# A pair of 64-row matmuls moved behind the convolution's visits, and into layer 1, in an S4D and channel-MLP kernel

## The chip, the core and the metric

The kernel runs on one core of a Trainium2 chip. The metric is the device time of one execution in microseconds (us). TensorE is called PE here, VectorE DVE, ScalarE ACT, GpSimd POOL and SyncE SP, as in the profile. A matmul has weights (the stationary operand, at most 128x128) and a moving operand whose columns stream past them; the profile writes the shape of the weights ahead of the matmul's own shape, as in `64*128 64x512`.

## The reference

```python
x = A_u                                   # (1, 2048, 576)
xn = layernorm(x)
# s: state-space convolution, per channel, with a kernel K made from 128 complex states
A = -exp(log_A_real) + 1j * A_imag;  C = (C_real + 1j * C_imag) * dt[:, None]
K = 2 * einsum("dn,dnl->dl", C, exp(A * dt * pos)).real
s = irfft(rfft(xn, 2L) * rfft(K, 2L))[:L] + xn * D_skip
# g: silu of a channel MLP, 576 -> 4608 -> 576
h = gelu(layernorm(xn) @ w1 + b1)
g = silu(h @ w2 + b2)
return x + s * g
```

All of it is float32.

## The kernel before

**The MLP.** It is most of PE's work. It runs in 48 slots: two halves of the tokens, in each 12 groups of 384 hidden columns, in each two blocks of 512 tokens. Float32 operands are split into a high and a low part, so that a product takes three matmuls (high x high, low x high, high x low). Layer 1 of a slot (L633) has three blocks of 128 hidden columns (i = 0, 1, 2). The contraction over 576 channels is four chunks of 128 rows, three matmuls each, and a rest of 64 rows. For the rest, `XR` holds the high part of the tokens in rows 0 to 63 and the low part in rows 64 to 127. One matmul with the weights `w1r` (the high part, twice) and one with `w1s` (the low part, twice) finish the block: 14 matmuls of 512 columns in all. Behind each block ACT takes gelu (L671) and the high part `hh` (L674), and DVE takes the low part `hl` (L677). Layer 2 (L707) multiplies these with `w2` in 72 matmuls of 288 columns, for four tiles of 128 tokens, and DVE adds each tile to `acc` (L717). Two PSUM buffers, `mxa` and `mxb`, alternate.

**The pair.** Of the `w1s` matmul only the 64 rows of the weights' low part by the tokens' high part are needed. A pair (L616) does that for blocks 0 and 2 of a slot by two matmuls of 64 rows side by side: one reads rows 0 to 63 of `XR`, the other a copy of them in rows 64 to 127 of `XQ` (named `bias` in the profile), fetched by a DMA in the slot before. These two start blocks 0 and 2, which then have 13 matmuls each. Pairs are made only where a slot begins behind a visit to the convolution, and stand ahead of that visit.

**The convolution** uses the PSUM buffer `cv`, in small matmuls that come as visits between blocks of the MLP. A visit has one or two segments of these kinds: kgen (L1042, weights of 128x32, 36 of them), x1 (L1157, 64x128, 12), k1 (L1188, 32x128, 12), s2 (L1217, 64x32, 24), inv (L1260, 32x64, 12), i1 (L1286, 128x64, 6). ACT and DVE take the results out and prepare the next operands.

**The order.** `Order` writes out the order of each engine's instructions beforehand, with its own clock and durations, and pins it. `pe_turns`, called behind blocks of the MLP, decides whether a visit stands there: by `EDGE`, `END`, `ALONE` and `DUE`, and by the positions at which visits are looked for (`all_lines`). `ride` puts a waiting kgen into another visit. `HOLD` names single steps of ACT and DVE that are traced one or two instructions later on their engine than the planner would have them.

**The end.** In the last slots, outputs are finished tile by tile: ACT takes the silu (L802), DVE multiplies (L809 or L811 and L815) and adds `u` (L820), DMAs store. The first half of the outputs comes out by `combine`: POOL's queue loads three tiles of rows (L746 to L748), DVE multiplies and adds (L754, L755), POOL's queue stores (L758). For the last chunk of channels this is done in three sets, of 3, 3 and 2 tiles, each behind the set before it, from the moment the last i1 is stored (L1295).

Of the kernel before, what the change touches and what calls it, by code (L numbers as in the profile page):

```python
# [18 lines left out]
P = 128  # L19
# [13 lines left out]
G = 3  # L33
# [191 lines left out]
def mixer_kernel(ctx, tc, u, log_a_real, a_imag, c_real, c_imag, log_dt, d_skip, w1, b1, w2, b2,  # L225
                 f1, f2, g2, g1, tvals, ident, out, parts=("mlp", "s4d")):
    nc = tc.nc
# [6 lines left out]
    def bank2(name):  # L234
        return ps.tile([P, 2, TB], F32, name=name, bufs=2 if name == "cv" else 1)
# [165 lines left out]
    MV, SECOND, PAIR, M4, SINGLE = {}, [], {}, [], {}  # L401
# [70 lines left out]
    XR = sb.tile([P, 2, TB], F32R, name="XR")  # L472
    XQ = {}
# [58 lines left out]
    W = {}  # L532
# [56 lines left out]
    HID, LAST, Q1, Q2, IDM = {}, {}, {}, {}, []  # L589
    turn = [0]  # L590

    def mx(i):
        return "mxa" if (turn[0] + i) % 2 == 0 else "mxb"

    BEGUN = set()
# [10 lines left out]
            XQ[0] = sb.tile([P, D], F32R, name="bias2")[:, :TB]  # L606
        nc.sync.dma_start(XQ[0][64:].bitcast(F32), XR[:64, tb].bitcast(F32))

    def pair(tb):

        Q1[0] = bank2(mx(1))
        for e, x in enumerate((XR[:64, tb], XQ[0][64:])):
            r, k = slice(64 * e, 64 * e + 64), e * (G - 1)
            nc.tensor.matmul(Q1[0][:, e], W[1][3][r, k * P:(k + 1) * P], x, start=True, stop=False,  # L616
                             skip_group_check=True)
        BEGUN.update((0, G - 1))

    def layer1(g, tb, i):  # L620
        h, lo, r1, r2 = W[1]
# [331 lines left out]
    def tables(b):  # L953
# [37 lines left out]
        def weigh(part):  # L991
# [10 lines left out]
            else:  # L1002
# [14 lines left out]
                + [step("DVE", dve((2, 2, 1, 1)[part] * n), f(weigh, part), need=[("sin", b, 1)],  # L1017
                        mark=("wu", b) if part == 3 else None, hold=HOLD.get(("weigh", b, part), 0)) for part in range(4)])

# [49 lines left out]
        return behind  # L1069


    X1, S2, INV, I1, KG = 1.5, 1.75, 2.15, 3.05, 1.03

    HOLD = {("weigh", 19, 3): 1, ("phase", 19): 1, ("frac", 18): 2, ("k", 2, 1): (2, 1), (2, 0, 24): 1, (2, 1, 24): 1, ("k1", 2, 1, 2): 1}

    def chunk(c):

# [240 lines left out]
    NPOS = G + 8  # L1318
    NSLOT = 4 * NG
    od = Order(tc, nc)  # L1320
    od.pinned = True
    el, wl2, wl, nl2, pl, pl2, nl, ml, ml2, xl, wx, c3, c2, c1, c4, kl, tl, sl, vl, gl, odl, fl = [od.line() for _ in range(22)]
    nlh, mlh, mlt = od.line(), od.line(), od.line()
    od.lines = od.lines[-3:] + od.lines[:-3]

# [75 lines left out]
    od.pin()  # L1401


    L1 = 14 * 0.2315
    LEN = [L1] * G + [3 * n * 0.132 + 0.02 for n in (4, 2, 2, 4, 3, 3, 3, 3)]

    T0 = 12.5
    for e, t in dict(PE=0.0, ACT=4.6, DVE=3.7, POOL=3.8, SP=0.0).items():
# [98 lines left out]
    def wmark(n, which):  # L1507

        per = KB + 1 + G
        a = n * per + (0 if which == 1 else KB + 1)  # L1510
        return [("w", k) for k in range(a, a + (KB + 1 if which == 1 else G))]
# [63 lines left out]


    pace = dict(left=NCH * (2 + 2 + 4), last=0.0, started=False)
    END = 1000.0


    EDGE = 0.2, 0.6
    ALONE, DUE = 20.0, (160.0, 950.0)

    def pe_turns(limit=1, any_time=False, all_lines=True, edge=None):
        for x in (nl, pl, ml) + ((c3, c1, kl) if all_lines else ()):
            n = 0
            while n < (2 if x in (c1, nl) else limit):
                h = od.head(x)
                if h is None or h[0]["eng"] != "PE" or h[1] > od.t["PE"] + (0.3 if x is nl else -0.4):
                    break  # L1590
                if x is c1:
                    now = od.t["PE"]
                    gap = (END - now) / max(pace["left"], 1)
                    if n == 0 and pace["started"] and now < pace["last"] + EDGE[edge is None] * gap and not any_time:
                        break
                    pace["started"], pace["last"] = True, now
                    pace["left"] -= 1
                if x is kl and pace["started"]:
                    b = kl["steps"][0]["mark"][1]
                    wait = ("wu", b + 1) not in od.marks or od.t["PE"] < DUE[0] + b * (DUE[1] - DUE[0]) / NB  # L1600
                    if b < NB - 1 and od.t["PE"] < h[1] + (ALONE if wait else 3.0):
                        break
                if edge is not None and not BEGUN and x in (c3, c1, kl):
                    m = wmark(edge // 2, 1) + [("xq", edge)]
                    if all(k in od.marks and od.marks[k] < od.t["PE"] - 0.3 for k in m):
                        od.unit(lambda: pair(edge % 2), 0.24)
                behind = ride(h[0]) if x in (c1, c3) else None
                od.run(x)
                if behind:
                    behind()  # L1610
                od.pin()
                od.advance(od.t["PE"])
                n += 1

    LATER = {}

    def later(slot, pos, f):
# [53 lines left out]
    for slot in range(NSLOT):  # L1671
        turn[0] = slot + 1
        od.shared = slot > 1
        g, tb = slot // 2 % NG, slot % 2
        n = slot // 2
        final = slot >= NSLOT - 2
        for pos in range(NPOS):
            if pos < G:
# [9 lines left out]
                if pos == 2:  # L1688
                    BEGUN.clear()
                    k = slot % (2 * NG)  # L1690
# [16 lines left out]
            else:  # L1707
# [13 lines left out]
                if halves:  # L1721
                    dh = terms[0][1]
                    od.marks["z", dh] = od.t["PE"] + od.LAT
                    x = od.line()
# [3 lines left out]
                if split:  # L1728
                    add = cell[0]
                    for d in range(2) if j == 0 else (terms[0][1],):  # L1730
                        m = ("acc", slot, j, d)
# [3 lines left out]
                        x = od.line()  # L1735
# [3 lines left out]
                if last and not halves:  # L1739
# [4 lines left out]
                    elif final:  # L1744
                        x = el if slot < NSLOT - 1 else od.line()
# [12 lines left out]
            for f in LATER.get((slot, pos), ()):  # L1758
                f()
            od.advance(od.t["PE"])  # L1760
            pe_turns(edge=slot + 1 if pos == NPOS - 1 else None, all_lines=pos in (0, 1, 2, G + 1, G + 3, G + 5, NPOS - 1))
    od.force(lambda: not od.urgent and not any(x["steps"] for x in od.lines))


# [52 lines left out]
```

## Time and profile before

| | before |
|---|---|
| median of 3 runs | 1095.55 us (1095.23 to 1095.94) |
| the profiled execution | 1095.67 us, of which its span 1093.9 us |
| granted PE clock | 0.999 |
| PE busy | 1087.1 us, 99% |
| DVE, ACT, POOL busy | 891.9 us (82%), 727.1 us (66%), 188.4 us (17%) |
| chain that ended last | PE 95%, DVE 3%, ACT 1% |
| pairs (L616) | 16 |

Matmuls overlap: of two in a row the second starts long before the profile's end of the first, so what a matmul costs PE is read from start to start and not from its duration. In the timeline, rows of one kind are merged (`x4`), and the first number is the start of the first of them.

### The profile page before, as it was taken

How to read it: one execution, taken by the hardware profiler on the slowest of the kernel's cores; microseconds unless marked ns; L12 is line 12 of the kernel's file. 1: busy time of each engine (PE TensorE's matmuls, PEld its weight loads, DVE VectorE, ACT ScalarE, POOL GpSimd, SP SyncE). 2: the span in 40 equal slices, each digit the busy share in tenths (PEclk: the TensorE clock that was granted, in tenths of full speed). 3: DMA queues.
4: the chain of work that ended last, by engine and by line, in shares of the span. 5: the costliest groups of instructions: out<-in, count | busy, mean ns of one | idle time of the engine just before them, and what ended most of it. 6: DMA issues, size and time to landing. Idle time of an engine off the chain costs nothing.

```text
span 1093.9 us, 27052 instructions
## 1 busy us (share of the span) xinstructions
PE 1087.1 (99%) x11445; PEld 954.0 (87%) x11445; DVE 891.9 (82%) x1302; ACT 727.1 (66%) x1113; POOL 188.4 (17%) x261
## 2 busy tenths in 40 slices
PE   9999999999999999999999999999999999999998
PEld 7989899899888898888988888888888888888897
DVE  7798667889998879889899987997969888766367
ACT  6585699778676674767767848685675757534333
POOL 4566210153020100001100000000001021101132
PEclk9999999999999999999999999999999999999999
DMA  8746764626354152355624215143142434454444
GB/s 242 225 149 152 236 235 143 179 80 157 116 160 134 44 112 67 96 110 148 161 48 118 78 56 141 34 122 87 56 126 42 144 101 132 114 170 150 137 151 103
DMA packets 139553, 138.22 MB, mean 126 GB/s; under 512 B 88952, under 2 KB 105016, under 8 KB 138856
## 3 DMA queue, kind: packets, MB, share of 16 engines
q1 hardware_dynamic: 124424, 85.05, 29.0%
q0 software_dynamic: 14528, 50.71, 14.7%
q8 instruction: 89, 1.46, 0.6%
q10 hardware_dynamic: 480, 0.74, 0.3%
q14 instruction: 32, 0.26, 0.1%
HBM read 102.17 MB, written 36.63 MB: 127 GB/s over the span
## 4 chain that ended last, share of the span: by engine, by line
PE 95%; DVE 3%; ACT 1%; SPq 1%; issue 0%; DMA 0%; POOL 0%; DVEq 0%; ACTq 0%; POOLq 0%
PE mxb L707 20%; PE mxa L707 20%; PE mxa L633 20%; PE mxb L633 20%; PE cv L1217 3%; PE cv L1042 3%; PE cv L1260 2%; PE cv L1286 2%; PE cv L1188 1%; PE cv L1157 1%; PE mxa L1348 1%; DVE acc L717 0%; PE mxa L648 0%; SPq L1089 0%; PE mxb L616 0%
## 5 line engine op out<-in xcount | busy, mean ns | idle before, releaser
L677 DVE TENSOR_TENSOR hl<-h,hh 128x512 fp32r<-128x512 f32 x144 | 98.5, 687 | 99.2 <-ACT hh L674 98.4
L707 PE MATMUL mxa<-w2h,hh 128*128 128x288 f32 x573 | 170.3, 297 | 0.0
L707 PE MATMUL mxb<-w2h,hh 128*128 128x288 f32 x573 | 170.2, 297 | 0.0
L707 PE MATMUL mxb<-w2h,hl 128*128 128x288 f32 x573 | 169.3, 295 | 0.1
L707 PE MATMUL mxa<-w2h,hl 128*128 128x288 f32 x573 | 169.1, 295 | 0.0
L707 PE MATMUL mxa<-w2l,hh 128*128 128x288 f32 x573 | 168.6, 294 | 0.0
L707 PE MATMUL mxb<-w2l,hh 128*128 128x288 f32 x573 | 168.6, 294 | 0.0
L671 ACT ACTIVATE h<-mxa,b1t 128x512 f32<-128x512 f32 x73 | 50.1, 687 | 98.3 <-PE mxa L633 95.1
L707 PEld LDWEIGHTS mxa<-w2h,hh 128*128 128x128 f32 x573 | 107.6, 188 | 5.8 <-issue 3.0
L707 PEld LDWEIGHTS mxb<-w2h,hh 128*128 128x128 f32 x573 | 107.6, 188 | 4.3 <-issue 1.4
L707 PEld LDWEIGHTS mxb<-w2l,hh 128*128 128x128 f32 x573 | 107.6, 188 | 0.8
L707 PEld LDWEIGHTS mxa<-w2l,hh 128*128 128x128 f32 x573 | 107.6, 188 | 0.6
L707 PEld LDWEIGHTS mxb<-w2h,hl 128*128 128x128 f32 x573 | 107.5, 188 | 0.3 <-DVE hl L677 0.3
L707 PEld LDWEIGHTS mxa<-w2h,hl 128*128 128x128 f32 x573 | 107.5, 188 | 0.0
L671 ACT ACTIVATE h<-mxb,b1t 128x512 f32<-128x512 f32 x71 | 48.8, 687 | 69.7 <-PE mxb L633 67.2
L674 ACT ACTIVATE hh<-h 128x512 fp32r<-128x512 f32 x144 | 90.7, 631 | 3.7
L944 POOL DMA_DIRECT2D par<-par_s x36 | 27.8, 771 | 367.8 <-DVE mg L988 325.0
L717 DVE TENSOR_TENSOR acc<-mxa,acc 128x576 f32<-128x576 f32 x87 | 65.5, 753 | 26.0 <-PE mxa L707 25.9
L717 DVE TENSOR_TENSOR acc<-mxb,acc 128x576 f32<-128x576 f32 (+1 forms) x89 | 65.9, 741 | 17.8 <-PE mxb L707 17.7
L633 PE MATMUL mxa<-XH,w1h 128*128 128x512 f32 x284 | 79.2, 401 | 0.0
L633 PE MATMUL mxb<-XH,w1h 128*128 128x512 f32 x280 | 77.7, 399 | 0.0
L633 PE MATMUL mxa<-XL,w1h 128*128 128x512 f32 x284 | 76.1, 390 | 0.0
(277 smaller groups left out, 2494.4 us busy)
## 6 DMA issues: line engine op xcount, KB each, us to landing
raw<-in_B_w_dram SPq DMA_DIRECT2D x72, 288.0 KB, 3.4
raw<-in_B_w_dram SPq DMA_DIRECT2D x96, 192.0 KB, 3.5
par_s<-A POOLq DMA_DIRECT2D x4, 2160.0 KB, 8.1
par<-par_s POOLq DMA_DIRECT2D x36, 240.0 KB, 3.6
f2t<-f2q SPq DMA_DIRECT2D x24, 256.0 KB, 3.6
g2t<-g2p SPq DMA_DIRECT2D x24, 256.0 KB, 4.1
bias<-XR SPq DMA_DIRECT2D x42, 128.0 KB, 3.6
raw<-in_B_w_dram SPq DMA_DIRECT2D x48, 96.0 KB, 3.7
```

The costliest lines, as they stand in the source:

```text
L633: nc.tensor.matmul(q, a, b, start=j == 0 and i not in BEGUN, stop=j == len(ops) - 1, skip_group_check=True)
L671: nc.scalar.activation(t, q, AF.Gelu_apprx_tanh, bias=b1t[:, k:k + 1], scale=1.0)
L674: LAST[0] = nc.scalar.activation(hh[:, i], t, AF.Copy)
L677: nc.vector.tensor_sub(hl[:, i], t, hh[:, i].bitcast(F32))
L707: nc.tensor.matmul(q[:, dh, :288], a[:, i, c], b[:, i, d], start=i == 0 and k == 0 and alone != 1, stop=i == G - 1 and k == 2, skip_group_ ...
L717: nc.vector.tensor_add(o, q[:, dh:dh + n, :288], b)
L944: nc.gpsimd.dma_start(PAR[b].rearrange("p (g i) k -> p g (i k)", g=4), dram(par_s, (b // 3 * 48 + b % 3 * 4) * NPAR, [[D * NPAR, P], [12 * ...
L1042: nc.tensor.matmul(q[32 * g:32 * g + 32, i // 2, i % 2 * 64:i % 2 * 64 + 64], U[:, ri, 4 * g + i, :], v[:, ri, 4 * g + i, :], start=ri == ...
L1157: nc.tensor.matmul(Q[24 * v][:, e], FP[0][r, f, 0], x[r, 12 * e:12 * e + 12], start=n == 0, stop=n == 2, skip_group_check=True)
L1217: nc.tensor.matmul(Q[i][32 * q:32 * q + 32, f, ri::2], m[r, 4 * i + q, 32 * ri:32 * ri + 32], A2[r, 4 * p + 2 * i + q // 2, :, :, q % 2], ...
L1260: nc.tensor.matmul(QI[q // 2][64 * f:64 * f + 64, q % 2, i], MAT["g2t", p + i // 2][r, i % 2, f, ri], YS[p + i // 2][0][r, i % 2, ri, f], ...
L1286: nc.tensor.matmul(Q[h][64 * y:64 * y + 64, t], g1t.rearrange("p a e -> p (a e)"), A2[:, k:k + 2, 1].rearrange("p i d r -> p i r d"), star ...
```

## The change

The pair now stands behind the visit and no longer ahead of it. It is also made within layer 1: where a visit stands behind block 0, a pair starts blocks 1 and 2 of the same slot. The planner takes 0.29 us for it, where it took 0.24 us. Beside this, nearly all settings of the order are new and `HOLD` is empty, so that visits stand in other places throughout the kernel; two lines of the planner (c2, c3 and c4, kl) change rank, and visits are no longer looked for at position G + 5.

```diff
-    def pair(tb):
+    def pair(tb, i):
-        Q1[0] = bank2(mx(1))
-        for e, x in enumerate((XR[:64, tb], XQ[0][64:])):
-            r, k = slice(64 * e, 64 * e + 64), e * (G - 1)
-            nc.tensor.matmul(Q1[0][:, e], W[1][3][r, k * P:(k + 1) * P], x, start=True, stop=False,
+        Q1[i] = bank2(mx(1))
+        for e, k, q, x in ((0, i, Q1[i][:, 0], XR[:64, tb]), (1, 2, Q1[0][:, 1], XQ[0][64:])):
+            nc.tensor.matmul(q, W[1][3][64 * e:64 * e + 64, k * P:(k + 1) * P], x, start=True, stop=False,
                              skip_group_check=True)
-        BEGUN.update((0, G - 1))
+        BEGUN.update((i, 2))
...
-    X1, S2, INV, I1, KG = 1.5, 1.75, 2.15, 3.05, 1.03
-    HOLD = {("weigh", 19, 3): 1, ("phase", 19): 1, ("frac", 18): 2, ("k", 2, 1): (2, 1), (2, 0, 24): 1, (2, 1, 24): 1, ("k1", 2, 1, 2): 1}
+    X1, S2, INV, I1, KG = 1.3, 1.73, 2.23, 2.96, 1.1
+    HOLD = {}
...
-    el, wl2, wl, nl2, pl, pl2, nl, ml, ml2, xl, wx, c3, c2, c1, c4, kl, tl, sl, vl, gl, odl, fl = [od.line() for _ in range(22)]
+    el, wl2, wl, nl2, pl, pl2, nl, ml, ml2, xl, wx, c2, c3, c1, kl, c4, tl, sl, vl, gl, odl, fl = [od.line() for _ in range(22)]
...
-    END = 1000.0
-    EDGE = 0.2, 0.6
-    ALONE, DUE = 20.0, (160.0, 950.0)
-    def pe_turns(limit=1, any_time=False, all_lines=True, edge=None):
+    END = 1005.0
+    EDGE = 0.01, 0.21
+    ALONE, DUE = 24.3, (97.0, 926.0)
+    PAIR, SOLO = (0.46, 0.29), False
+    def pe_turns(limit=1, any_time=False, all_lines=True, edge=None, to=None, inner=False):
+        away = 0
...
-                if edge is not None and not BEGUN and x in (c3, c1, kl):
-                    m = wmark(edge // 2, 1) + [("xq", edge)]
-                    if all(k in od.marks and od.marks[k] < od.t["PE"] - 0.3 for k in m):
-                        od.unit(lambda: pair(edge % 2), 0.24)
+                away += x in (c3, c1, kl)
                 behind = ride(h[0]) if x in (c1, c3) else None
                 od.run(x)
...
+        if (away or inner and SOLO) and to is not None and not BEGUN:
+            m = wmark(to // 2, 1) + [("xq", to)]
+            if all(k in od.marks and od.marks[k] < od.t["PE"] - 0.3 for k in m):
+                od.unit(lambda: pair(to % 2, int(inner)), PAIR[away > 0])
+    TURNS = 0, 1, 2, G + 1, G + 3, NPOS - 1,
...
-            pe_turns(edge=slot + 1 if pos == NPOS - 1 else None, all_lines=pos in (0, 1, 2, G + 1, G + 3, G + 5, NPOS - 1))
+            pe_turns(edge=slot + 1 if pos == NPOS - 1 else None, all_lines=pos in TURNS,
+                     to=slot if pos == 0 else slot + 1 if pos == NPOS - 1 else None, inner=pos == 0)
```

**What the programs hold.** PE's order has the same 102 segments of the convolution in both, in 74 visits before and 76 now. There are 16 pairs before and 29 now, 23 of these at a slot's start and 6 behind block 0. A pair stands directly beside x1, whose weights have the same shape as the pair's, in 5 of the 16 places before and in 3 of the 29 now (a visit of x1 and kgen begins with x1 and ends with kgen). The other neighbours on the visit's side are s2, inv, k1, i1 and kgen, whose weights have other shapes. Of the 144 matmuls with `w1s`, 32 are halves of pairs before and 58 now; no matmul is added or left out.

The first place is on PE, at the start of a slot with s2 in the visit (about 296 us into the span before; `f2t` and `A` are s2's operands). Before:

```order
L707 MATMUL mxa<-w2h,hl 128x288
L616 MATMUL mxb<-XR,w1s 128x512
L616 MATMUL mxb<-bias_773,w1s 128x512
L1217 MATMUL cv<-A_83,f2t 32x2x96 x32
L633 MATMUL mxb<-XH,w1h 128x512 x4
L633 MATMUL mxb<-XL,w1h 128x512 x4
```

and now:

```order
L705 MATMUL mxa<-w2h,hl 128x288
L1215 MATMUL cv<-A_83,f2t 32x2x96 x32
L614 MATMUL mxb<-XR,w1s 128x512
L614 MATMUL mxb<-bias_773,w1s 128x512
L631 MATMUL mxb<-XH,w1h 128x512 x4
L631 MATMUL mxb<-XL,w1h 128x512 x4
```

The pair went from between layer 2 and the visit to between the visit and layer 1; a line number is two lower in the changed kernel.

The second place is on PE too, in layer 1 of an earlier slot, behind a kgen (about 232 us into the span before). Before:

```order
L633 MATMUL mxa<-XR,w1s 128x512
L1042 MATMUL cv<-w 32x64 x32
L633 MATMUL mxb<-XH,w1h 128x512 x4
L633 MATMUL mxb<-XL,w1h 128x512 x4
L633 MATMUL mxb<-XH,w1l 128x512 x4
L633 MATMUL mxb<-XR,w1r 128x512
L633 MATMUL mxb<-XR,w1s 128x512
```

and now:

```order
L631 MATMUL mxa<-XR,w1s 128x512
L1040 MATMUL cv<-w 32x64 x32
L614 MATMUL mxb<-XR,w1s 128x512
L614 MATMUL mxa<-bias_773,w1s 128x512
L631 MATMUL mxb<-XH,w1h 128x512 x4
L631 MATMUL mxb<-XL,w1h 128x512 x4
L631 MATMUL mxb<-XH,w1l 128x512 x4
L631 MATMUL mxb<-XR,w1r 128x512
```

The pair is new here; block 1 (and block 2, further down) ends a matmul earlier.

The third place is on DVE, at the end of the program, from the additions of the last tiles on (`A` holds the convolution's result, `w` the outputs). Before:

```order
L717 TENSOR_TENSOR acc<-cv,acc 128x288
L820 TENSOR_TENSOR w<-w,A_83 128x576
L809 SCALAR_TENSOR_TENSOR A_83<-A_83,h_13134 128x288
L809 SCALAR_TENSOR_TENSOR A_83<-A_83,h_13156 128x288
L820 TENSOR_TENSOR w<-w,A_83 128x576
```

and now:

```order
L715 TENSOR_TENSOR acc<-cv,acc 128x288
L752 TENSOR_TENSOR row<-row 128x384
L753 TENSOR_TENSOR row<-row 128x384
L818 TENSOR_TENSOR w<-w,A_83 128x576
L807 SCALAR_TENSOR_TENSOR A_83<-A_83,h_13130 128x288
L807 SCALAR_TENSOR_TENSOR A_83<-A_83,h_13155 128x288
L818 TENSOR_TENSOR w<-w,A_83 128x576
```

The last set of `combine` (L752, L753; L754, L755 before) stood between two `hl` of the last layer 1, and now stands among the last outputs. The last i1, from which the sets follow, stood within layer 2 of the fourth slot from the end, behind its first 18 matmuls, and now stands at that slot's end.

## Rows read from the trace of the kernel before

**Rows 1.** The page's section of busy time (share of the span) and instructions.

```profile
PE 1087.1 (99%) x11445; PEld 954.0 (87%) x11445; DVE 891.9 (82%) x1302; ACT 727.1 (66%) x1113; POOL 188.4 (17%) x261
```

**Rows 2.** Timeline of PE, within a layer 1 block: start, length, engine, line, operation.

```profile
375.67 1.07 PE L633 MATMUL mxb<-XH,w1l 128*128 128x512 f32 x4
376.58 0.39 PE L633 MATMUL mxb<-XR,w1r 128*128 128x512 f32 x1
```

**Rows 3.** Timeline of PE, a visit of s2 alone within layer 2.

```profile
997.72 0.29 PE L707 MATMUL mxa<-w2l,hh 128*128 128x288 f32 x1
997.85 0.29 PE L707 MATMUL mxa<-w2h,hl 128*128 128x288 f32 x1
998.08 1.62 PE L1217 MATMUL cv<-A,f2t 64*32 64x192 f32 x64
999.62 0.40 PE L707 MATMUL mxb<-w2h,hh 128*128 128x288 f32 x1
999.86 0.30 PE L707 MATMUL mxb<-w2l,hh 128*128 128x288 f32 x1
```

**Rows 4.** Timeline of PE, a pair ahead of s2.

```profile
296.11 0.29 PE L707 MATMUL mxa<-w2h,hl 128*128 128x288 f32 x1
296.32 0.50 PE L616 MATMUL mxb<-XR,w1s 64*128 64x512 f32 x1
...
296.76 1.60 PE L1217 MATMUL cv<-A,f2t 64*32 64x192 f32 x64
```

**Rows 5.** Timeline of PE, a pair ahead of x1, and layer 1 behind.

```profile
250.22 0.29 PE L707 MATMUL mxa<-w2h,hl 128*128 128x288 f32 x1
250.44 0.50 PE L616 MATMUL mxb<-XR,w1s 64*128 64x512 f32 x1
...
250.78 0.52 PE L1157 MATMUL cv<-pr,f2t 64*128 64x384 f32 x4
251.13 0.51 PE L1157 MATMUL cv<-ys,f2t 64*128 64x384 f32 x4
251.48 0.51 PE L1157 MATMUL cv<-pr,f2t 64*128 64x384 f32 x4
251.93 1.20 PE L633 MATMUL mxb<-XH,w1h 128*128 128x512 f32 x4
```

**Rows 6.** Timeline of PE, a visit of x1 alone within layer 2.

```profile
549.33 0.29 PE L707 MATMUL mxa<-w2h,hl 128*128 128x288 f32 x1
549.54 0.62 PE L1157 MATMUL cv<-pr,f2t 64*128 64x384 f32 x4
550.00 0.52 PE L1157 MATMUL cv<-ys,f2t 64*128 64x384 f32 x4
```

**Rows 7.** Timeline of DVE, the last outputs.

```profile
1085.97 0.46 DVE L717 TENSOR_TENSOR acc<-cv,acc 128x288 f32<-128x288 f32 x1
1086.35 0.75 DVE L820 TENSOR_TENSOR w<-w,A 128x576 f32<-128x576 f32 x1
1087.01 0.82 DVE L809 SCALAR_TENSOR_TENSOR A<-A,h 128x288 f32<-128x288 f32 x2
1087.87 0.76 DVE L820 TENSOR_TENSOR w<-w,A 128x576 f32<-128x576 f32 x1
1088.55 0.45 DVE L809 SCALAR_TENSOR_TENSOR A<-A,h 128x288 f32<-128x288 f32 x1
...
1089.89 0.46 DVE L820 TENSOR_TENSOR w<-w,A 128x288 f32<-128x288 f32 x1
```

**Rows 8.** Timeline of DVE, the last set of combine.

```profile
1077.65 0.55 DVE L754 TENSOR_TENSOR row<-row 128x384 f32<-128x384 f32 x1
```

**Rows 9.** Timeline of POOL, that set's four stores.

```profile
1079.09 2.12 POOL L758 DMA_DIRECT2D out_dram<-row  x4 [12.83 <-DVE row L755]
```

**Rows 10.** Timeline of PE, the longest wait among layer 2's matmuls.

```profile
567.86 0.29 PE L707 MATMUL mxb<-w2l,hh 128*128 128x288 f32 x1
568.24 0.40 PE L707 MATMUL mxb<-w2h,hl 128*128 128x288 f32 x1
```

More of the change, by code (lines that the diff above doesn't have):

```diff
@@ L1401, in mixer_kernel @@
     od.pin()
-    L1 = 14 * 0.2315
-    LEN = [L1] * G + [3 * n * 0.132 + 0.02 for n in (4, 2, 2, 4, 3, 3, 3, 3)]
+    L1 = 14 * 0.2317
+    LEN = [L1] * G + [3 * n * 0.1319 + 0.02 for n in (4, 2, 2, 4, 3, 3, 3, 3)]
     T0 = 12.5
@@ L1588, in pe_turns @@
                 h = od.head(x)
-                if h is None or h[0]["eng"] != "PE" or h[1] > od.t["PE"] + (0.3 if x is nl else -0.4):
+                if h is None or h[0]["eng"] != "PE" or h[1] > od.t["PE"] + (0.3 if x is nl else -0.07):
                     break
```

## Prediction, made before the changed kernel ran

> **What bounds the kernel.** I read the page's busy times first: PE is busy for 99% of the span [rows 1], and in the chain of work that ended last it has 95%. So it matters what PE does and how long it stands still, and, behind PE's last matmul, the chain of the last outputs. A busy share of 99% could still hide waits, since the profile models a matmul's end, so I went through PE's timeline from start to start. A pass of 512 columns in layer 1 takes 0.227 us: four of them lie 0.91 us apart [rows 2]. A pass of 288 columns in layer 2 takes 0.13 us [rows 3]. These steps repeat nearly everywhere. The longest wait among layer 2's matmuls is a step of 0.38 us in place of 0.13 us [rows 10], and there are few others. The kernel is therefore close to a plain sum of PE's passes, and what else costs time is the change from one shape of weights to another. That is the thing to price.
>
> **A change of shape.** A visit of s2 alone shows it [rows 3]. From layer 2's last matmul to s2's first it takes 0.23 us where an ordinary step takes 0.13 us: 0.10 us more, in which the last pass runs out before weights of another shape are loaded. Behind the visit, layer 2's first matmul is followed by its second after 0.24 us in place of 0.13 us: 0.11 us more, in which the first weights of the new shape are loaded with nothing beside them. One change costs 0.21 us. A visit has one change more than it has segments of different shapes: one into each and one back.
>
> **The pair as it stands before.** A pair's weights are 64 rows by 128 columns, and its two matmuls run side by side, so it is one pass. It replaces two passes of layer 1, 2 x 0.227 = 0.455 us. What it adds, ahead of s2: from layer 2's last matmul to s2's first it takes 0.65 us [rows 4], without a pair 0.23 us [rows 3], so 0.42 us. That is a pass of 0.227 us and a change of 0.21 us, since neither layer 2 nor s2 has the pair's shape. Ahead of x1, which has the pair's shape, it is less: to x1's second group it takes 0.91 us [rows 5], without a pair 0.67 us [rows 6], so 0.24 us, a pass and nothing more. So a pair gains 0.455 - 0.42 = 0.03 us beside another shape and 0.455 - 0.24 = 0.21 us beside x1. In the kernel before, 5 of the 16 stand beside x1: 5 x 0.21 + 11 x 0.03 = 1.4 us gained.
>
> **The pairs as they stand now.** No row shows a pair behind a visit, so I build it from its neighbours. The way from the visit's last matmul to the next shape is there with or without a pair; with it, it leads to the pair. Then comes the pair's load with nothing beside it (0.11 us, as for layer 2's first matmul in [rows 3]), its pass (0.227 us), and the step from its shape to layer 1's. For that step there is a row: x1 has the pair's shape, its groups lie 0.35 us apart, and layer 1 starts 0.45 us behind the last group [rows 5], 0.10 us more. The sum is 0.11 + 0.227 + 0.10 = 0.44 us, practically the 0.42 us of a pair ahead of a visit; I take 0.43 us. It matters little at which side of the visit the pair stands: its shape has to be entered and left. Only behind x1 is it entered for nothing, for 0.24 us. Of the 29 pairs now, 3 stand there: 3 x 0.21 + 26 x 0.025 = 1.3 us gained, against 1.4 us before. **The pairs: +0.1 us.** Thirteen more of them, and no more gained, as two of the good places are lost (visits of x1 and kgen end with kgen). The bounds of one behind another shape: 0.24 us, if it is entered as cheaply as behind x1, and 0.44 us. I take the upper end, since five other shapes next to it (s2, inv, k1, i1, kgen) come at the price of a change in the kernel before, of which s2 is shown.
>
> The Trainium skill, TensorEngine Tiling (Array Packing), Tiling Modes, says that a change of the tiling mode, other than one from tile to tile, drains TensorE. By that rule a pair behind a visit pays for it as one ahead does, and the sum stays as it is. The same page's Overview promises up to twice the speed for 64 rows; with nothing lost at the edges the sum would be that of the first rival below.
>
> **The visits.** The segments are the same 102. There are 76 visits now and 74 before, so two more ways back: 2 x 0.21 us. **+0.4 us.** PE's blocks of the MLP are the same, apart from the passes counted above.
>
> **The end.** The last i1 stands later by most of a slot's layer 2, and with it the three sets of combine, whose last one now stands on DVE among the last outputs (third place in the order). Before, it stood between two `hl`, where DVE had time. Now its two operations stand ahead of the second last tile's output. The first took 0.55 us [rows 8], and the second does the same over the same shape: 1.1 us. DVE has no room there: from the addition at 1085.97 us on, each row starts within 0.04 us of the end of the one before, up to the fifth, and the last ends at 1090.35 us [rows 7]; what lies between are outputs of the last tile that came the same way. Everything behind it, with ACT's store of the last half tile, moves by what is put in. **+1.1 us.** It would cost nothing if that chain had a gap that I don't see; it can't gain. POOL's queue now has the set's four stores between its own last ones: issued from 1087.5 us on, in 2.1 us [rows 9], with the two behind them in 1.1 us more, they are out by 1090.7 us, ahead of DVE's last output, which would then end at 1091.4 us. They add nothing.
>
> **Waits.** DVE and ACT get a new order in the middle of the kernel, and I can't read waits from an order. The steps of the one long wait cost 0.25 us, and 0.11 us more for the load behind it [rows 3, 10]: 0.36 us. It may go: -0.4 us. On the other side, `HOLD` is emptied, which had put eight steps behind one or two others; if each of them now gives such a wait, that is 8 x 0.36 = 2.9 us. I take zero, as the two planners leave the same work to DVE, and the one before kept PE free of waits with DVE at 82%.
>
> **The sum.** 0.1 + 0.4 + 1.1 + 0 = +1.6 us. The profiled execution took 1095.67 us, 0.1 us over the median of the runs; 1095.55 + 1.6 gives 1097.2 us, 0.15% slower. A measurement of this kernel can tell about 0.2%, 2.2 us, from no change, so this is "within", near its upper edge.
>
> **Rivals.** *The pair behind a visit is nearly free of changes.* If it is entered with the visit's own way back, it adds 0.24 us everywhere: 29 x 0.21 = 6.1 us gained, 4.7 us more than before. With +0.4 and +1.1 us that makes 1092.3 us. The planner's own 0.29 us would give 29 x 0.165 = 4.8 us, so 3.4 us more, and 1093.7 us. For it speaks only that nothing in the trace shows the place itself; against it, that x1 to layer 1, a change between just these shapes, costs 0.10 us at its end, and that s2 alone pays at both ends. Chance 0.18.
>
> *VectorE's row of work delays `hl`.* In the trace the long wait stands before a matmul of layer 2 that reads `hl` [rows 10], and PE waits whenever DVE has put two transposes or a table's step ahead of it. Without the holds both transposes of x1 in the third chunk of channels stand together ahead of an `hl`. At 0.36 us each, the second such wait makes the kernel slower than can be missed (1097.2 + 0.7 = 1097.9 us); with all eight it is 1100.1 us, and I put it at 1098.6 us. For it speaks DVE's load; against it, that layer 1 leaves an `hl` of the first two blocks several us. Chance 0.22.
>
> *The end has room.* If DVE's two operations slip in where it waits for ACT, the kernel takes 1096.1 us. Chance 0.05. The forecast as worked out has 0.55.
>
> **How the numbers follow.** Slower by over 0.2% (beyond 1097.74 us): the second rival and a small part of the forecast's own spread, 0.22 + 0.08 = 0.30. Faster by over 0.2% (below 1093.36 us): most of the first rival, 0.13. Within: the rest, 0.57. The range leaves out the cheaper half of the first rival and the upper half of the second, about 0.2 together: 1093.0 to 1099.2 us.
>
> **What the profile after would show.** Pairs are right if, from a pair to layer 1's first matmul, there are about 0.43 us where s2, inv, k1, i1 or kgen precede it, and about 0.33 us behind x1, and if the step into the pair is as long as from the same segment to layer 1. They are wrong if it is 0.24 us. The end is right if DVE's last output ends 1.1 us later behind PE's last matmul than before. Waits are right if no step within layer 2 is over 0.4 us and there are not many of them. The forecast fails if changes of shape cost less in this direction, or if a new wait repeats in every chunk of channels.

## The result, and the profile after

| | before | after |
|---|---|---|
| median of 7 runs | 1095.55 us (1095.23 to 1096.19) | 1098.87 us (1098.71 to 1099.54) |
| ratio, 95% interval | | 1.0031 (1.0019 to 1.0043) |
| the profiled execution | 1095.67 us | 1098.75 us |
| its span | 1093.90 us | 1096.97 us |
| PE's last matmul starts | 1088.56 us | 1088.44 us |
| DVE's last output ends | 1090.35 us | 1091.29 us |
| last store lands | 1092.98 us | 1095.62 us |

The kernel is 0.31% slower, 3.3 us. The forecast was 1.6 us. The page's busy times after, which answer to [rows 1]:

```profile
PE 1087.0 (99%) x11445; PEld 951.6 (87%) x11445; DVE 891.8 (81%) x1302; ACT 724.6 (66%) x1111; POOL 188.5 (17%) x261
```

PE does the same work in the same time. Its last matmul, in the timeline of PE, before and then after:

```profile
1088.56 0.29 PE L707 MATMUL cv<-w2h,hl 128*128 128x288 f32 x1
```

```profile
1088.44 0.29 PE L705 MATMUL cv<-w2h,hl 128*128 128x288 f32 x1
```

PE ends 0.12 us earlier than before. So in these two executions the whole loss lies behind PE's last matmul, and it has three parts. From that matmul to the end of DVE's last output it takes 2.85 us in place of 1.79 us (+1.06). From there to the last landing it takes 4.33 us in place of 2.63 us (+1.70). From there to the end of the span it takes 1.35 us in place of 0.92 us (+0.43). With PE's -0.12 that is the difference of the spans, 3.07 us.

The first part in the timeline of DVE after, the last outputs, which answer to [rows 7, 8]:

```profile
1085.86 0.45 DVE L715 TENSOR_TENSOR acc<-cv,acc 128x288 f32<-128x288 f32 x1
1086.23 0.55 DVE L752 TENSOR_TENSOR row<-row 128x384 f32<-128x384 f32 x1
1086.81 0.56 DVE L753 TENSOR_TENSOR row<-row 128x384 f32<-128x384 f32 x1
1087.28 0.75 DVE L818 TENSOR_TENSOR w<-w,A 128x576 f32<-128x576 f32 x1
...
1090.83 0.46 DVE L818 TENSOR_TENSOR w<-w,A 128x288 f32<-128x288 f32 x1
```

The two operations of `combine` (L752, L753) stand between the addition at 1085.86 us and the output at 1087.28 us, where before the output followed the addition after 0.38 us; now it is 1.42 us. The second part begins on POOL's queue. Its timeline, before and then after (the latter answers to [rows 9] too):

```profile
1085.73 1.08 POOL L826 DMA_DIRECT2D out_dram<-w  x2 [0.29 <-POOL w L820]
1087.39 1.04 POOL L826 DMA_DIRECT2D out_dram<-w  x2 [0.58 <-DVE w L820]
```

```profile
1085.61 1.11 POOL L824 DMA_DIRECT2D out_dram<-w  x2 [0.29 <-POOL w L818]
1087.67 2.09 POOL L756 DMA_DIRECT2D out_dram<-row  x4 [0.94 <-DVE row L753]
1089.74 1.05 POOL L824 DMA_DIRECT2D out_dram<-w  x2
```

The four stores of the last set take 2.09 us (2.12 us before), and POOL's last two stores of outputs go out behind them, at 1089.74 and 1090.26 us in place of 1087.39 and 1087.91 us. They now come within the stores that SP and ACT issue at the end. The DMA view of those last stores (line, queue, count, KB of each, median us from issue to landing), before from 1087.3 us on and after from 1089.55 us on:

```profile
out_dram<-w POOLq DMA_DIRECT2D x2, 144.0 KB, 2.5
out_dram<-w SPq DMA_DIRECT2D x2, 144.0 KB, 2.4
out_dram<-w ACTq DMA_DIRECT2D x2, 72.0 KB, 2.3
out_dram<-w SPq DMA_DIRECT2D x2, 72.0 KB, 2.6
```

```profile
out_dram<-w SPq DMA_DIRECT2D x2, 144.0 KB, 2.4
out_dram<-w POOLq DMA_DIRECT2D x2, 144.0 KB, 3.5
out_dram<-w ACTq DMA_DIRECT2D x2, 72.0 KB, 4.1
out_dram<-w SPq DMA_DIRECT2D x2, 72.0 KB, 4.2
...
```

The same eight stores, 864 KB, are issued in 3.15 us before (1087.39 to 1090.54) and in 2.15 us after (1089.59 to 1091.74), and the last four land 4.1 and 4.2 us after their issue in place of 2.3 and 2.6 us. (These are medians of two, or the one that the trace has: in both executions two of the eight stores, one each of SP and ACT, have no landing on record.) What the DMA engines do in that stretch is in the DMA view's rows of busy tenths (40 slices) and of packets, before from 1088.6 to 1092.3 us and after from 1090.6 to 1095 us:

```profile
DMA  9296601789899196999599677776979989996576
...
DMA packets 546, 0.82 MB, mean 223 GB/s; under 512 B 118, under 2 KB 365, under 8 KB 546
```

```profile
DMA  0894979997995336949989796987995955766441
...
DMA packets 581, 0.88 MB, mean 200 GB/s; under 512 B 136, under 2 KB 389, under 8 KB 581
```

They are busy most of the time in both, and move 223 and 200 GB/s. Before, the stores come at 864 KB in 3.15 us, 281 GB/s, not much more than the engines move. After, they come at 411 GB/s, twice what the engines move. As I read it, the stores issued last wait until the others' bytes are through.

### The profile page after: what moved, and what is told of

It is laid out like the page before. It is cut to its first block, busy times and chain, and to the rows that moved or that the text cites. A ratio compares the mean times of both kernels' runs of the same rounds, so it can differ in the third digit from the quotient of the medians.

```text
span 1097.0 us, 27052 instructions
## 1 busy us (share of the span) xinstructions
PE 1087.0 (99%) x11445; PEld 951.6 (87%) x11445; DVE 891.8 (81%) x1302; ACT 724.6 (66%) x1111; POOL 188.5 (17%) x261
## 4 chain that ended last, share of the span: by engine, by line
PE 98%; DVE 1%; issue 0%; ACT 0%; POOL 0%; DVEq 0%; POOLq 0%
PE mxb L705 21%; PE mxa L705 21%; PE mxa L631 21%; PE mxb L631 20%; PE cv L1040 3%; PE cv L1215 3%; PE cv L1258 2%; PE cv L1284 2%; PE cv L1186 1%; PE cv L1155 1%; PE mxa L1346 1%; PE mxb L614 1%; PE mxa L614 0%; PE mxa L646 0%; PE cv L516 0%; DVE A L807 0%
## 5 line engine op out<-in xcount | busy, mean ns | idle before, releaser
L705 PE MATMUL mxb<-w2h,hh 128*128 128x288 f32 x573 | 169.9, 297 | 0.0
L715 DVE TENSOR_TENSOR acc<-mxa,acc 128x576 f32<-128x576 f32 x87 | 65.4, 752 | 20.2 <-PE mxa L705 20.2
L715 DVE TENSOR_TENSOR acc<-mxb,acc 128x576 f32<-128x576 f32 (+1 forms) x89 | 65.9, 741 | 15.0 <-PE mxb L705 14.7
```

The costliest lines, as they stand in the source:

```text
L705: nc.tensor.matmul(q[:, dh, :288], a[:, i, c], b[:, i, d], start=i == 0 and k == 0 and alone != 1, stop=i == G - 1 and k == 2, skip_group_ ...
L715: nc.vector.tensor_add(o, q[:, dh:dh + n, :288], b)
```

## The experiments

All comparisons with before are on the same chip; the changed kernel has no run on these chips, so its own time is compared by its ratio to before, 1.0031 (1.0019 to 1.0043). "PE's body" is the time from the first layer 1 matmul of the fourth slot to PE's last matmul, which leaves out the start of the program: 1016.18 us before, 1016.12 us after. "Tail" is DVE's end behind PE's last matmul, and "landing" the last landing behind DVE's end: 1.79 and 2.63 us before, 2.85 and 4.33 us after.

### The end: is it POOL's queue?

Theory: DVE's two operations cost 1.06 us, and POOL's four stores another 1.7 us, since they bring POOL's last stores among the others. Rival: only DVE's two operations count and the rest is chance of that execution or belongs to the new order on PE.

**e1_last_set_early.** The last set starts 6 us of the planner's clock earlier.

```diff
-                ml["steps"].append(step(None, 13.0, lambda a=a: combine_load(*a), ...
+                ml["steps"].append(step(None, 7.0 if b == 6 else 13.0, lambda a=a: combine_load(*a), ...
```

> The changed kernel, with one number of the order changed: the last set of combine is held back 7 us behind its loads in the planner's clock, and not 13 us, so that its two DVE operations stand behind the last hl and its four stores ahead of POOL's last ones, as in the kernel before. Theory (a jam of stores at the end: 0.9 us from DVE's two operations, and 2 us since the set's four stores hold up those behind them): 1098.87 - 2.9 = 1096.0 us, the last store of ACT lands 2.3 us after its issue again. Rival 1 (only DVE's operations count, the late landing has another cause): 1098.0 us, landing stays at 4.1 us. Rival 2 (the time is lost in PE's visits and not at the end): no change, 1098.9 us.

Measured: 1096.60 us, 1.0012 (1.0002 to 1.0021) of before's 1095.26 us. The edit moved more than the set: with the new number the planner also put the last two visits elsewhere on PE, an inv and the last i1. The i1 is back within layer 2, where the kernel before has it, and the pair behind it is gone, so that 28 pairs are left. In the timeline of PE, after and then in this run:

```profile
1027.90 2.92 PE L1284 MATMUL cv<-A,g1t 128*64 128x384 f32 x16
```

```profile
1023.96 2.92 PE L1284 MATMUL cv<-A,g1t 128*64 128x384 f32 x16
```

So this run alone doesn't isolate the set; e2 and e11, whose order on PE is that of after, do. Landing is 2.50 us, near before's 2.63 us. The tail is 2.20 us, not 1.79 us: 0.4 us are lost in a way that I had not thought of. The timelines of POOL and then of DVE in this run:

```profile
1083.01 2.13 POOL L756 DMA_DIRECT2D out_dram<-row  x4 [6.90 <-DVE row L753]
1085.16 1.45 POOL L818 TENSOR_TENSOR w<-w,A 128x576 f32<-128x576 f32 x1
```

```profile
1086.02 1.21 DVE L807 SCALAR_TENSOR_TENSOR A<-A,row 128x576 f32<-128x576 f32 x1
```

The four stores now stand ahead of POOL's own addition of an output (L818). It starts at 1085.16 us, 4.15 us ahead of PE's last matmul in this run; after, it starts at 1083.87 us, 4.57 us ahead of PE's last matmul. It is 0.42 us late. DVE's multiplication beside it (1086.02) takes 1.21 us; the same one took 0.79 us after, where POOL was nearly done.

**e2_no_set_stores.** After, with the four stores of the last set left out (that part of the output is not written), DVE's two operations kept in their place.

```diff
-        for i in range(n):
+        for i in range(n if b != 6 else 0):
             for y, o in enumerate(rows_at(out, b + i, c0, c1)):
                 nc.gpsimd.dma_start(o, x[64 * y:64 * y + 64, i])
```

> The changed kernel without the four stores of the last set of combine (their part of the output is left out); DVE's two operations stay where they are. Theory (jam): the stores behind them land 2.3 to 2.7 us after their issue, 1098.87 - 2.0 = 1096.9 us. Rival 1 (late landing has another cause): 1098.8 us. Rival 2 (all 3.2 us come from DVE and the order): 1098.8 us.

Measured: 1097.24 us, 1.0019 (1.0009 to 1.0029). That is 2.0 us over before, 1.3 us less than the changed kernel's 3.3 us. The tail is 2.84 us, as after, and landing is 2.50 us, near before's 2.63 us. In the runs below that keep the four stores where they are after (e4, e5 and e6), landing is 4.28 to 4.34 us again. So the four stores are the cause of the second part, and DVE's operations alone are not.

**e11_set_stores_on_sp.** Takes the bytes from the queue: the same four stores of 48 KB, issued by SP.

```diff
-                nc.gpsimd.dma_start(o, x[64 * y:64 * y + 64, i])
+                (nc.sync if b == 6 else nc.gpsimd).dma_start(o, x[64 * y:64 * y + 64, i])
```

> The changed kernel, only that the four stores of the last set of combine are issued by SP and not by POOL; DVE's operations stay among the last outputs. Theory (the jam comes from POOL's own last two stores, which can only be issued behind the set's four, 1.3 us later than in the run with the late set in the kernel before, and then land together with SP's and ACT's last ones): POOL's last stores are issued about 1.5 us earlier, and the last store lands 2.5 us behind DVE's end as before; 1097.2 us. Rival (too many bytes at the end, whichever queue issues them): the last store lands 4 us behind DVE's end, 1098.8 us.

Measured: 1097.31 us, 1.0013 (1.0004 to 1.0023) of before's 1095.91 us. The DMA view of this run, all stores from 1088.5 us on (the first of SP's four was issued just ahead):

```profile
out_dram<-w POOLq DMA_DIRECT2D x2, 144.0 KB, 2.5
out_dram<-w SPq DMA_DIRECT2D x2, 144.0 KB, 2.6
out_dram<-row SPq DMA_DIRECT2D x4, 48.0 KB, 2.6
out_dram<-w ACTq DMA_DIRECT2D x2, 72.0 KB, 2.3
out_dram<-w SPq DMA_DIRECT2D x2, 72.0 KB, 2.3
```

The bytes are the same as after, but POOL's two stores go out at 1088.98 and 1089.50 us, the first 0.11 us ahead of PE's last matmul and not 1.30 us behind it, and all twelve take from 1088.04 to 1092.66 us, 1056 KB in 4.6 us, 235 GB/s. (After, all twelve come at 266 GB/s, from 1087.67 to 1091.74 us, and only the last eight at 411 GB/s.) They land after 2.3 to 2.6 us (medians). So it isn't the 192 KB; it is when POOL's last two stores go out, and how closely the stores follow each other. Landing is 3.06 us only since SP's own last store goes out 0.7 us behind DVE's end, held by the row of issues on its queue. That is the price of moving them to SP.

**e3_before_set_late.** The same from the other side: before, with the last set started 8 us of the planner's clock later.

```diff
-                ml["steps"].append(step(None, 13.0, lambda a=a: combine_load(*a), ...
+                ml["steps"].append(step(None, 21.0 if b == 6 else 13.0, lambda a=a: combine_load(*a), ...
```

> The kernel before, with the last set of combine held back 21 us and not 13 us, so that its DVE operations stand among the last outputs (one place ahead of where the changed kernel has them) and its four stores between POOL's last ones. Pairs, visits and all else are those of before. Theory (jam): 1095.55 + 2.9 = 1098.5 us, PE's last matmul starts at the same time as before. Rival 1 (the changed kernel's end is late through its later i1 and later loads of s): 1095.55 + 1.0 = 1096.6 us, as DVE's operations alone would give. Rival 2 (the loss is in the visits): 1095.6 us.

Measured: 1096.38 us, 1.0009 (1.0000 to 1.0019), where I expected 1098.5. The tail is 2.97 us (+1.18), landing 2.53 us. The set's operations came out one place earlier on DVE than after, so the stores started 1.72 us ahead of PE's last matmul (0.77 us after), and POOL's last two went out at 1088.44 and 1088.96 us: eight stores in 2.9 us, 306 GB/s, and no landing on record over 2.9 us (that of SP's last store is not on record). It repeats the first part, DVE's operations, and not the second. In the order of how fast the 864 KB are issued, 281 (before), 306 (e3) and 411 GB/s (after), the longest landing goes 2.7, 2.9 and 4.5 us.

### The pairs: what does one cost, and where?

Theory: a pair costs 0.43 us behind a visit of another shape and 0.24 us behind x1, against 0.455 us that it saves. Rival: it is cheaper behind a visit, or the visits themselves became dearer.

What the trace of after says by itself, first a pair behind x1 and then one behind x1 and kgen (timeline of PE):

```profile
251.56 0.52 PE L1155 MATMUL cv<-pr,f2t 64*128 64x384 f32 x4
251.91 0.39 PE L614 MATMUL mxb<-XR,w1s 64*128 64x512 f32 x1
...
252.25 1.18 PE L631 MATMUL mxb<-XH,w1h 128*128 128x512 f32 x4
```

```profile
270.81 0.29 PE L705 MATMUL mxb<-w2h,hl 128*128 128x288 f32 x1
...
272.28 1.10 PE L1040 MATMUL cv<-w 128*32 128x64 f32 x64
273.32 0.50 PE L614 MATMUL mxa<-XR,w1s 64*128 64x512 f32 x1
...
273.74 1.19 PE L631 MATMUL mxa<-XH,w1h 128*128 128x512 f32 x4
```

In the first, the pair follows x1's last group after 0.35 us, as x1's groups follow each other, and layer 1 comes 0.34 us later. In the second, the pair is followed by layer 1 after 0.42 us. A visit with a pair less the same visit without one, in e4 below at the same place, is 0.23 to 0.24 us for x1 (3 places), 0.40 to 0.45 us for s2, k1, inv, i1 and x1 with kgen, and behind kgen alone 0.43 us twice and 0.74 us once, where half of the pair waited for 0.31 us.

By their medians the four runs that follow can't be told from the kernel that they change; what they show of the pairs rests on their traces, place for place.

**e4_no_pairs.** After, in the same order, with the pairs' work back in layer 1's fourteenth matmul.

```diff
     def pair(tb, i):
+        BEGUN.update((i, 2))
+        return
...
-        if i not in BEGUN:
-            ops.append((r2[:, c], XR[:, tb]))
+        ops.append((r2[:, c], XR[:, tb]))
...
```

> The changed kernel with the same order on all engines, but without any pair: the blocks of layer 1 have all 14 matmuls. Theory (a pair costs a pass and a change of shape, 0.43 us, beside any shape but x1's, 0.23 us beside x1, and saves 0.455 us): PE's last matmul starts 29 x 0.455 - 26 x 0.43 - 3 x 0.23 = 1.3 us later, 1100.2 us. Rival 1 (a pair behind a visit costs the planner's 0.29 us): 4.8 us later, 1103.7 us. Rival 2 (a pair is worse than none, through waits): earlier than 1098.9 us.

Measured: 1099.66 us, 1.0042 (1.0027 to 1.0057). PE's body is 1017.10 us, 0.98 us over after's; the tail and landing are after's (2.85 and 4.28 us). So 29 pairs gain 1.0 us. That is the sum of the visits' prices as well: 29 x 0.455 = 13.20 us saved, 12.24 us added.

**e5_pairs_ahead.** After, with the 23 pairs at a slot's start put ahead of the visit, in the same order otherwise.

```diff
...
+        if edge in AHEAD:
+            pair(edge % 2, 0)
+            BEGUN.clear()
+            od.pin()
         for x in (nl, pl, ml) + ...
...
-                od.unit(lambda: pair(to % 2, int(inner)), PAIR[away > 0])
+                od.unit(lambda: pair(to % 2, int(inner)) if inner else BEGUN.update((0, 2)), PAIR[away > 0])
```

> The changed kernel with the same order on all engines, only that the 23 pairs at a slot's start stand ahead of their visit again; the 6 within layer 1 stay behind theirs. Theory (a pair costs a pass and a change of shape on either side, and no change beside x1): four visits of x1 and kgen have x1 beside the pair again, 4 x 0.2 = 0.8 us less on PE, the others are the same; 1098.1 us. Rival (behind a visit a pair is cheaper, 0.29 us against 0.42 us): 17 x 0.13 = 2.2 us more, less 0.8 us for x1: 1100.3 us.

Measured: 1098.78 us, 1.0027 (1.0017 to 1.0037). PE's body is 1015.78 us, 0.34 us under after's: the four visits give 0.76 us, and a visit of kgen and s2 at 446 us, without a pair, took 0.36 us longer in this execution. The visit shown above, now with the pair ahead of x1:

```profile
270.64 0.29 PE L705 MATMUL mxb<-w2h,hl 128*128 128x288 f32 x1
270.86 0.50 PE L614 MATMUL mxa<-XR,w1s 64*128 64x512 f32 x1
...
271.20 0.52 PE L1155 MATMUL cv<-pr,f2t 64*128 64x384 f32 x4
...
273.38 1.20 PE L631 MATMUL mxa<-XH,w1h 128*128 128x512 f32 x4
```

From layer 2's last matmul to layer 1 it takes 2.74 us in place of 2.93 us. This holds for the four visits of x1 with kgen; at the other places a pair costs 0.43 to 0.475 us ahead. Directly beside x1 a pair is cheap on either side; elsewhere the side makes little difference.

**e8_before_pairs_behind.** Before, with its 16 pairs behind the visit.

```diff
...
-                        od.unit(lambda: pair(edge % 2), 0.24)
+                        od.unit(lambda: BEGUN.update((0, G - 1)), 0.24)
+                        late = True
...
+        if late:
+            pair(edge % 2)
+            od.pin()
```

> The kernel before with the same order on all engines, only that its 16 pairs stand behind their visits. Theory: 13 pairs cost the same, the 3 behind x1 and kgen lose x1 as neighbour, 3 x 0.2 = 0.6 us more on PE: 0.6 us over the kernel before on the same chip. Rival (behind is cheaper): 11 x 0.13 = 1.4 us less, with the 0.6 us: 0.8 us under the kernel before.

Measured: 1096.22 us, 1.0004 (0.9995 to 1.0013): the move alone can't be told from no change. In the trace its pairs cost 0.48 us more than before's, place for place; three visits of x1 with kgen are 0.18 us dearer each, and the others are the same.

**e6_kgen_ahead_of_x1.** After, with the kgen that rides in a visit of x1 put ahead of x1's matmuls, so that the pair follows x1.

```diff
         def x1(i):
+                lead(q)
                 for n, (f, x) in enumerate(((0, a), (0, b), (1, a))):
...
-                lead(q)
```

> The changed kernel, only that in a visit of x1 and kgen the kgen comes first, so that x1 stands beside the pair in seven of the 29 places and not in three. Theory (shape of the neighbour decides): each of the four costs 0.23 us and not 0.43 us, 0.8 us less on PE, 1098.1 us. Rival (it is x1 itself or the place ahead of the visit that made the pair cheap, not the neighbour's shape): no change, 1098.9 us.

Measured: 1098.44 us, 1.0022 (1.0012 to 1.0031). The same visit:

```profile
271.05 0.29 PE L705 MATMUL mxb<-w2h,hl 128*128 128x288 f32 x1
...
272.30 0.62 PE L1156 MATMUL cv<-pr,f2t 64*128 64x384 f32 x4
...
273.46 0.39 PE L614 MATMUL mxa<-XR,w1s 64*128 64x512 f32 x1
...
273.79 1.18 PE L631 MATMUL mxa<-XH,w1h 128*128 128x512 f32 x4
```

It takes 2.74 us again, and the pairs now gain 1.8 us together, 0.8 us more than after, nearly all of it in the four visits; PE's body is 1015.08 us, 1.04 us under after's. This is the size of the one good place: each pair that finds x1 beside it is worth 0.2 us, the others 0.02 us.

### Both mended

**e12_end_and_kgen.** After, with the edits of e1, e6 and e11 together: the last set early, its stores on SP, kgen ahead of x1.

> The changed kernel with three of the edits above at once: kgen ahead of x1 in their common visits, the last set of combine held back 7 us and not 13 us, and its four stores issued by SP, so that POOL's addition of the last slot's first tile isn't held up by them and doesn't share a time with DVE's last chain. Theory: 1.0 us less on PE, 1.0 us less in DVE's chain, 1.8 us less for the landing: 1098.87 - 3.8 = 1095.1 us, 0.2 to 0.8 us under the kernel before on the same chip. Rival 1 (the early set costs elsewhere what it gains at the end, as in the run with the early set alone, whose end was 0.4 us longer than that of before): 1095.6 us or more, the same as before. Rival 2 (the changed kernel's places of visits lose time beyond pairs and end): 1097 us.

Measured: 1095.48 us, 1.0002 (0.9993 to 1.0011) of before's 1095.45 us, where I expected 0.2 to 0.8 us under it. The tail is 1.79 us and landing 2.90 us; SP's last store goes out 0.49 us behind DVE's end here, 0.19 us before, and why isn't known. As in e1, the last i1 is back within layer 2 and 28 pairs are left. With the set's stores on SP, POOL's addition is back in its place, and DVE's multiplication beside it too (timelines of POOL and DVE):

```profile
1083.39 1.46 POOL L818 TENSOR_TENSOR w<-w,A 128x576 f32<-128x576 f32 x1 [8.63 <-PE mxa L705]
```

```profile
1084.67 0.79 DVE L807 SCALAR_TENSOR_TENSOR A<-A,row 128x576 f32<-128x576 f32 x1
```

So the three edits together undo the loss: two of them mend the end, and the third takes 0.8 us off the visits. The new order, with 12 pairs more than before, is then as fast as before and no faster. PE's body is 1015.24 us; that of e3, which has before's order on PE, is 1015.16 us.

## Why the prediction was right or wrong, point by point

**The pairs (+0.1 us forecast): right.** I built the price behind another shape as 0.44 us from its neighbours and took 0.43 us; it is 0.40 to 0.45 us. Behind x1 I took 0.24 us, and it is 0.23 to 0.24 us. The 29 gain 0.96 us in the visits and 0.98 us in PE's body by e4, where I had 1.3 us; the wait of 0.31 us in one of them (below) is what is missing. Before's 16, held against e4's visits of the same kinds, gain 1.3 us, where I had 1.4 us. The difference is 0.3 us where I had 0.1 us, and without that wait it would be nothing. The first rival, a pair nearly free behind a visit, is out: it holds behind x1 alone, which is the place that I priced so. The Trainium skill, TensorEngine Tiling (Array Packing), Tiling Modes, says that a change of tiling mode drains TensorE; the 0.23 to 0.24 us without and the 0.40 to 0.45 us with such changes agree.

**The visits (+0.4 us): right.** Counted from the last matmul of the MLP ahead of a visit to the second one behind it, less the two ordinary steps, all visits with their pairs take 169.9 us in place of 163.3 us, 6.6 us more, and 13 pairs more save 5.9 us. That is +0.7 us on PE, 0.3 us of it the new wait below, where the first two terms together gave +0.5 us.

**Waits (0): right in size, and more is in this term than I saw.** Before's wait of [rows 10], 0.36 us with the load behind it, and one of 0.17 us at 482 us are gone, and with them most of what the visits cost more. No run of matmuls of layer 2 behind 51 us now takes over 0.06 us more than its passes, so the emptied `HOLD` cost nothing and the second rival is out, though its 1098.6 us is nearest to the measured time. One new wait is there, at the first pair within layer 1. The timelines of PE and then of ACT after:

```profile
233.15 0.50 PE L614 MATMUL mxb<-XR,w1s 64*128 64x512 f32 x1
233.46 0.50 PE L614 MATMUL mxa<-bias,w1s 64*128 64x512 f32 x1
```

```profile
231.42 1.28 ACT L669 ACT_TABLE_LOAD   x1
232.71 0.69 ACT L669 ACTIVATE h<-mxa,b1t 128x512 f32<-128x512 f32 x1
```

The two halves of a pair start within 0.02 us of each other everywhere else. Here the second starts 0.31 us later: it writes `mxa`, which ACT's gelu of block 0 still reads, and that gelu came late behind a load of its table. At 698 us, at the same kind of place, gelu was done by then and both halves start at 699.59 us. This wait belongs to the new order: all seven traces that have the pair show it, with 0.31 to 0.33 us, so the pair there costs 0.74 us and saves 0.455 us. Other waits do not: e3 has before's order on PE and shows neither of before's two waits, and its body is 1015.16 us in place of 1016.18 us; the two waits are 0.53 us of that, the rest lies in steps too small to name. So the second rival's sentence that PE waits whenever DVE has two transposes or a table's step ahead of an `hl` is too strong: at 568 us e3 has them there and doesn't wait. After's order on PE has a body of 1016.12 us, 1016.00 us in e2 and 1015.97 us in e11; e1, with two visits placed otherwise and one pair less, has 1016.53 us, with a wait of 0.4 us at 305 us that after, e2 and e11 don't show. Against e3, then, the new order costs PE 0.8 to 1.0 us, and against before nothing, as two executions of one order differ by up to 1.0 us: PE's -0.12 us in the two executions above doesn't show that the new order is free on PE, and the +0.7 us of the visits is the better measure.

**The end (+1.1 us): DVE's part right, the failed step behind it.** The chain is 1.06 us longer, by the two operations, with no gap to hide them, as the step said; e3 repeats it with before's order. The step that failed is the last of that paragraph: POOL's queue, with the set's four stores between its own last ones, is "out by 1090.7 us, ahead of DVE's last output", and "They add nothing". The issues were right (the last one goes from 1090.26 to 1090.79 us, and DVE's last output ends at 1091.29 us), the conclusion was not. I compared POOL's issues with DVE's end, and not the bytes with what the DMA engines move. POOL's last 288 KB fell into the same 2.15 us as the 576 KB of SP and ACT, and the six stores issued from 1090.1 us on were late, as far as their landings are on record (3.9 to 4.5 us): +1.70 us of landing. That they waited for the others' bytes is my reading; that the set's four stores on POOL's queue are the cause is shown by e2 and e11. The view for it was at hand: the DMA engines were busy in that stretch before as well. POOL's own addition matters too: e1 shows that the set can stand early only if its stores don't delay it, or 0.4 us come back on DVE.

**What is left open.** The stretch from the last landing to the span's end grew by 0.43 us, 0.92 to 1.35 us; it is between 0.93 and 1.35 us in the other runs, and no run was made for it. That the stores wait for the engines' rate is read from three rates of issue and their landings; no run changed the rate of issue alone. Why the engines moved 200 GB/s in after's last stretch and 223 GB/s in before's isn't known; 0.88 MB at before's rate would be 0.45 us faster. What the new order costs PE isn't known to better than some 0.5 us, as executions of one order differ by that and more. The old settings with the new pairs, and the new settings with the old ones, each planned by the kernel's own planner, were not tried.

**The verdict.** "Within 0.2%" had the largest chance, 0.57, but 1098.87 us lies beyond the 1097.74 us where I had put "slower", with 0.30. The range held the time by luck: its upper part stood for the second rival's waits, which didn't come, and not for late stores. The sign was right, the size half of what it is: +1.6 us against 3.3 us (2.1 to 4.7 by the interval). The landing of the last stores, +1.70 us, is the size of what is missing; the +0.43 us behind the last landing, which I had not foreseen either, is more than balanced by PE (-0.12 us in place of +0.5 us).

## What to carry to other kernels

Here a pass of narrow matmuls cost its pass and a change of shape more (0.43 us); beside matmuls of its own shape it cost the pass alone, and only there did the pair pay (0.2 us against 0.02 us). Before a planner is told a price for such a pass, price each neighbour apart. At a kernel's end, add up for every queue the bytes of the last stores and the time in which they are issued, and compare with what the DMA engines move; a queue that "is done before the last engine" can still put its bytes ahead of the last engine's. After an edit to a planned order, compare the whole order and not only the place that was meant: in e1 one number moved two visits and lost a pair.

## What the runs showed of the hardware that I had not expected

Stores of outputs at the end landed 2.3 to 2.7 us after their issue where 864 KB came at 281 GB/s (before), and where they came at 411 GB/s (after) the first two on record landed after 2.4 and 2.9 us and the later ones after 3.9 to 4.5 us, while the engines moved 223 and 200 GB/s.

DVE's operations with two operands in SBUF waited for POOL's addition. In after, e1 and e3, DVE's operation that started beside it ended at 1085.93, 1087.23 and 1085.38 us, and POOL's addition at 1085.32, 1086.61 and 1084.97 us: 0.61 and 0.62 us behind it for the multiplication over 576 columns (0.75 us when POOL adds nothing beside it, in e3), 0.41 us for an addition over 384 columns (0.55 us, [rows 8]). Each is the operation's own time less 0.14 us, however early DVE started. The rows of e3, POOL and then DVE:

```profile
1083.53 1.44 POOL L820 TENSOR_TENSOR w<-w,A 128x576 f32<-128x576 f32 x1 [17.73 <-DVE A L809]
```

```profile
1084.68 0.70 DVE L754 TENSOR_TENSOR row<-row 128x384 f32<-128x384 f32 x1
...
1086.26 0.75 DVE L809 SCALAR_TENSOR_TENSOR A<-A,row 128x576 f32<-128x576 f32 x1
```

DVE's additions out of PSUM in e1 (L715, 0.46 us at 1085.53 us, within POOL's addition) are no longer for it than elsewhere. The Trainium skill, SBUF — State Buffer, SBUF: two separate sides, says that DVE with two inputs in SBUF and a GpSimd operation that reads SBUF lock each other out, and that the later one waits; these rows agree, but for the 0.14 us.
